# FFN weight conversion in a fused attention, MoE and FFT-mixer kernel: the product written over the raw words, the low parts subtracted by VectorE

## The chip, the cores and the metric

The kernel runs on one core of a Trainium2 chip. The metric is device microseconds (us) of one execution, the median of several runs. Engines are named as in the profile: PE (TensorE), DVE (VectorE), ACT (ScalarE), POOL (GpSimd), SP (SyncE, here only an issuer of DMAs).

## The reference

Three blocks follow one another on data of 4 batches, 576 rows and 512 columns: an attention, a gated MLP ("MoE"), and a Fourier mixer with a feed-forward network (FFN). The change touches only the preparation of the weights of the last block:

```python
def _moe2_ref(x, w_ch1, w_ch2):
    X = np.fft.fft(x, axis=1)
    X = np.fft.fft(X, axis=2)
    u = x + np.real(X).astype(np.float32)
    ...
    un = (u - mu) / np.sqrt(var + 1e-06)
    ch = np.maximum(un @ w_ch1, 0.0) @ w_ch2     # w_ch1: 512 x 2048, w_ch2: 2048 x 512
    return (u + ch).astype(np.float32)
```

The weights are drawn with numpy's default type, so `w_ch1` and `w_ch2` lie in memory as 8-byte floats, two 32-bit words for each number.

## The kernel before

Every product that must be exact to float32 is split: a number is a high part (rounded to the matmul's `fp32r` format) plus a low part, and `mm3` (L138) issues three matmuls (L139 high x high, L140, L141 with one low part each).

**The FFN's weights.** They are cut into 32 pieces of 128 x 512 numbers, one of `w_ch1` and one of `w_ch2` for each of the 16 steps `f` of the hidden dimension. A piece is fetched by SP as 128 x 1024 raw words (L921 for `w_ch1`, L113 for `w_ch2`) into one of 4 `raw` buffers, which lie in the space of the later tiles `unh` and `unl`. `narrow` (L118) makes float32 of it: ACT multiplies the odd words (the upper halves, taken as float32) by 2^-112 into a tile (L124); DVE shifts and masks that into a second tile (L125), ORs the sign in (L126), and ORs the top bits of the even words in (L128, which reads `raw` a second time and so is the last reader of the buffer). `split` (L105) then lets ACT write the rounded high part into its final place (L106) and an engine given by name subtract to get the low part (L107). For the FFN's pieces this engine was POOL, set by `W1ENG` and `W2ENG` (L83, L84). Both temporary tiles come from the ring `t2`, 6 buffers that the Fourier stages use too; in the trace a buffer of it is named `t`.

**When a piece is converted.** The converted pieces lie in tiles of the earlier stages, as these are released: `p_winh`, `p_winl`, `p_wsh`, `p_wsl`, and after the last Fourier transform `p_wfh`, `p_wfl`, `p_dsh`, `p_dsl`, `p_xgh`, `p_xgl`, `p_vyh`, `p_vyl` and others. The generator `ffn_gen` offers conversions (`ahead`, up to 3 steps ahead; `ready_w`, what is due; `conv_here`, at fixed places of the last batch's Fourier stages). After a piece is converted the fetch of the piece 4 further on is issued into its raw buffer.

**The FFN around it.** The rows are worked in five blocks. Of the first block, step `f` runs 12 matmuls of 512 columns for the hidden values of step f+1 (`ch1`, into a PSUM bank `mm`); ACT writes their high part `hh` (relu, L589), DVE the low part `hl` (L977, reading PSUM and `hh`); then 12 or more matmuls (`ch2`) multiply the `hh` and `hl` of step f with `w_ch2` into banks named `tp` and `sc`. The Fourier transform of the last batch (its stages `even`, `odd` and `tail`, L710 to L729, where DVE L727 writes a part of `yh`, and `even_d`, `odd_d` with DVE L815 to L822) runs between the first steps of that block. Only the first block meets conversions; the other four reuse the pieces.

**What sets the order.** The program text gives the dependencies; a scheduler at build time then fixes the order of the instructions on every engine, from the dependencies, the rings and its own model. Each engine runs its list in that order, so an instruction that waits holds all that stand behind it on its engine.

Of the kernel before, what the change touches and what calls it, by code (L numbers as in the profile page):

```python
# [44 lines left out]
def tile_attn_moe_fft_mixer(  # L45
# [18 lines left out]
    nc = tc.nc  # L64
# [15 lines left out]

    LOENG = nc.gpsimd
    E = {x: nc.gpsimd if x in POOLOPS else nc.vector for x in ('vnl', 'gl', 'pd', 'vd', 'un', 'vt', 'e', 'ed', 'pd1', 'wfl', 'bf', 'bf2', 'ul')}
    W1ENG = nc.gpsimd  # L83
    W2ENG = nc.gpsimd  # L84

    def bank(tag, shape):
        n = 1
# [10 lines left out]
    def t2(n=512):  # L98
        t = tmp.tile([P, 610], F32, tag="t2", name="t2", bufs=T2)
        return t[:, :n]  # L100
# [16 lines left out]

    def narrow(raw, n, scratch=None):  # L118
        w = raw.rearrange("p (n two) -> p n two", two=2)
        m = t2(n) if scratch is None else scratch[0]  # L120
        mi = m.bitcast(I32)
        a = t2(n) if scratch is None else scratch[1]
        ai = a.bitcast(I32)
        nc.scalar.mul(m, w[:, :, 1], 2.0 ** -112)  # L124
        nc.vector.tensor_scalar(ai, mi, 3, 0x7FFFFFF8, op0=ALU.logical_shift_left, op1=ALU.bitwise_and)  # L125
        nc.vector.scalar_tensor_tensor(ai, in0=mi, scalar=-2 ** 31, in1=ai, op0=ALU.bitwise_and,  # L126
                                       op1=ALU.bitwise_or)
        nc.vector.scalar_tensor_tensor(ai, in0=w[:, :, 0].bitcast(I32), scalar=29, in1=ai,  # L128
                                       op0=ALU.logical_shift_right, op1=ALU.bitwise_or)
        return a  # L130

    def split_raw(hi, lo, raw, n, dbl, eng):
        a = narrow(raw, n) if dbl else raw
        if len(hi.shape) == 3:
            a = a.rearrange("p (k m) -> p k m", k=hi.shape[1])
        split(hi, lo, a, eng)
# [50 lines left out]
    def prep():  # L187
        dbl = wide(w_in)
        sg = big.tile([P, 4, 512], F32, tag="wfl", name="scratch")
        prev = None  # L190
        for n in range(8):
            h, kk = 1 - n // 4, n % 4
            c = slice(h * 512, (h + 1) * 512)
            w = stage[n][:, :512 * dbl]
            if dbl == 2:
                w = narrow(w, 512, (sg[:, 2 * (n % 2), :], sg[:, 2 * (n % 2) + 1, :]))
            hi = winh[:, kk, c]
            nc.scalar.copy(hi, w)
            if prev is not None:
                prep_lo(*prev)  # L200
            prev = (winl[:, kk, c], w, hi)
            yield
        prep_lo(*prev)
        yield
# [39 lines left out]
    def prep_late():  # L244
# [8 lines left out]
        for kk in range(4):  # L253
            raw = stgs[kk % 2][:, :512 * dbl]
            w = narrow(raw, 512, (sg[:, 0, :], sg[:, 1, :])) if dbl == 2 else raw
            f = sg[:, 2, :]
            nc.vector.tensor_scalar(f[:, 0:257:256], w[:, 0:257:256], 2.0, None, op0=ALU.mult)
            nc.vector.tensor_tensor(f[:, 1:256], w[:, 1:256], w[:, 511:256:-1], op=ALU.add)
            nc.vector.tensor_tensor(f[:, 257:512], w[:, 1:256], w[:, 511:256:-1], op=ALU.subtract)
            if kk < 2:  # L260
                fetch(stgs[kk][:, :512 * dbl], w_out[(kk + 2) * P:(kk + 3) * P, :], nc.sync)
            nc.scalar.mul(wfh[:, kk, :], f, 0.25)
            nc.vector.scalar_tensor_tensor(wfl[:, kk, :], in0=f, scalar=0.25, in1=wfh[:, kk, :].bitcast(F32),
                                           op0=ALU.mult, op1=ALU.subtract)
            yield 0.5
# [644 lines left out]
    def ffn_gen(ffn):  # L910
# [13 lines left out]
        def conv_w(f, which):  # L924
            hi, lo = (w1, w2)[which][f]
            split_raw(hi, lo, raws[2 * (f % 2) + which][:, :512 * wd], 512, wd == 2, W1ENG if which == 0 else W2ENG)

# [154 lines left out]
    n = early = 0  # L1082
# [105 lines left out]
```

## Time and profile before

| | |
|---|---|
| time, median of 3 runs | 863.43 us (863.38 to 864.03) |
| the profiled execution: time, span in the trace | 863.25 us, 861.1 us |
| PE busy | 806.6 us, 94% of the span |
| DVE busy | 487.3 us, 57% |
| ACT busy | 304.0 us, 35% |
| POOL busy | 190.2 us, 22% |
| the chain that ended last, by engine | PE 77%, DVE 10%, SP's queue 5%, issue 3%, DMA 3%, ACT 1%, POOL 1% |
| TensorE's granted clock, mean | 0.98 of full speed |

All times in the profile are in us from the start of the span unless they are marked ns. A share such as "DVE 57%" is a mean over the whole span; the change touches only the stretch from about 393 us (the first piece) to 516 us (the last). The chain that ended last is followed backwards from the last instruction, each time to what released it. A row of the timeline names the start, the duration, the engine, the source line, the operation and its tiles; the brackets at its end say how long the engine had been idle just before it and what ended that. Consecutive instructions of one engine overlap a little in the records (an instruction's record ends some 0.08 us after the next one's begins), so what an instruction costs its engine is the distance between two starts.

### The profile page before, as it was taken

The page shows a single profiled execution, that of the slowest core. Times are in us where ns is not written, and L with a number is a line of the kernel's source. Part 1 is how long each engine was busy: PE and PEld are TensorE (multiplying, and loading weights), DVE is VectorE, ACT ScalarE, POOL GpSimd, SP SyncE. Part 2 cuts the span into 40 slices and gives each one's busy share as a digit, 9 for nine tenths or more (in the row PEclk, how much of TensorE's full clock was granted, in tenths as well). Part 3 has the DMA queues.
Part 4 walks back from the last instruction along what each step waited for, and adds up shares of the span by engine and source line. Part 5 has one row for each costly group of instructions (what it writes and reads, how often), then busy time and mean ns, then how long its engine had stood idle before and what let it go on. Part 6 is the DMA issues. An engine that isn't in the chain of part 4 may idle for free.

```text
span 861.1 us, 14356 instructions
## 1 busy us (share of the span) xinstructions
PE 806.6 (94%) x5309; PEld 667.6 (78%) x5309; DVE 487.3 (57%) x1109; ACT 304.0 (35%) x929; POOL 190.2 (22%) x237
## 2 busy tenths in 40 slices
PE   3758999999999999999798889999999999999998
PEld 1546888778977897889687658888888888888897
DVE  3798899577577846679959994223222322221211
ACT  1764674546373717434542542111110111111111
POOL 4447532224122310033623551000000000000000
PEclk9977999999999999999999999999999999999999
DMA  7789364432333110051525652322121222110100
GB/s 121 178 181 192 73 130 126 83 88 46 70 54 99 34 46 1 19 190 49 155 91 165 195 163 60 108 50 59 40 98 40 59 50 83 40 25 0 49 1 25
DMA packets 154210, 71.84 MB, mean 83 GB/s; under 512 B 122806, under 2 KB 140823, under 8 KB 154141
## 3 DMA queue, kind: packets, MB, share of 16 engines
q1 hardware_dynamic: 152668, 65.63, 31.2%
q0 software_dynamic: 1472, 5.30, 1.9%
q8 instruction: 42, 0.69, 0.3%
q14 instruction: 28, 0.22, 0.1%
HBM read 58.83 MB, written 12.07 MB: 82 GB/s over the span
## 4 chain that ended last, share of the span: by engine, by line
PE 77%; DVE 10%; SPq 5%; issue 3%; DMA 3%; ACT 1%; POOL 1%; DVEq 0%
PE mm L139 15%; PE mm L140 14%; PE mm L141 14%; PE tp L141 4%; PE tp L139 4%; PE tp L140 4%; PE sc L139 3%; PE sc L140 3%; PE sc L141 3%; SPq L326 3%; DVE t L128 2%; PE sc L433 2%; SPq L354 2%; PE sc L481 1%; DVE t L125 1%
## 5 line engine op out<-in xcount | busy, mean ns | idle before, releaser
L977 DVE SCALAR_TENSOR_TENSOR hl<-mm,hh 128x512 fp32r<-128x512 f32 (+1 forms) x80 | 50.9, 637 | 222.0 <-ACT hh L589 221.9
L589 ACT ACTIVATE hh<-mm 128x512 fp32r<-128x512 f32 (+1 forms) x80 | 44.3, 554 | 273.8 <-PE mm L141 269.2
L599 POOL TENSOR_TENSOR rs<-ve,nhalf 128x1 f32<-128x1 f32 (+1 forms) x38 | 25.2, 676 | 254.2 <-DVE ve L598 250.1
L386 ACT ACTIVATE eb<-sc,mx 128x64 f32<-128x64 f32 x140 | 41.7, 339 | 32.8 <-DVE mx L384 32.8
L139 PE MATMUL mm<-xgh,winh 128*128 128x288 f32 x128 | 39.2, 307 | 0.0
L139 PE MATMUL mm<-wsh,vnh 128*128 128x288 f32 x128 | 38.5, 301 | 0.0
L140 PE MATMUL mm<-xgl,winh 128*128 128x288 f32 x128 | 38.2, 298 | 0.0
L141 PE MATMUL mm<-xgh,winl 128*128 128x288 f32 x128 | 38.1, 297 | 0.0
L140 PE MATMUL mm<-wsl,vnh 128*128 128x288 f32 x128 | 38.0, 297 | 0.0
L141 PE MATMUL mm<-wsh,vnl 128*128 128x288 f32 x128 | 38.0, 297 | 0.0
L406 DVE STREAM_TRANSPOSE qk<-qk 128x576 f32<-128x576 f32 x28 | 21.7, 775 | 25.0 <-DMA qk<-in_q_dram 14.0
L128 DVE SCALAR_TENSOR_TENSOR t<-raw,t 128x512 int32<-128x512 int32 x32 | 34.6, 1085 | 0.1
L386 ACT ACTIVATION_READ_ACCUMULATOR eb<-sc,mx 128x1 f32 x140 | 32.4, 232 | 0.0
L423 POOL TENSOR_TENSOR ta<-qk 128x288 f32<-128x288 f32 x28 | 22.9, 817 | 41.0 <-DVE qk L406 34.3
L139 PE MATMUL mm<-wfh,xgh 128*128 128x512 f32 (+1 forms) x76 | 31.5, 414 | 0.0
L140 PE MATMUL mm<-wfl,xgh 128*128 128x512 f32 (+1 forms) x76 | 30.3, 400 | 0.0
L829 POOL DMA_INDIRECT u_d<-t,idx x12 | 15.5, 1293 | 64.8 <-DVE t L822 58.7
L141 PE MATMUL mm<-wfh,xgl 128*128 128x512 f32 (+1 forms) x76 | 29.4, 402 | 0.0
L481 PE MATMUL sc<-qk 64*64 64x64 f32 x560 | 20.4, 246 | 8.5 <-DMA qk<-in_q_dram 3.9
L481 PEld LDWEIGHTS sc<-qk 64*64 64x64 f32 x560 | 16.3, 153 | 14.6 <-DVE qk L406 9.8
L139 PE MATMUL mm<-winh,xgh 128*128 128x512 f32 x64 | 26.6, 416 | 0.7 <-DVE t L803 0.6
L411 POOL TENSOR_TENSOR vp<-vp 72x512 f32<-72x512 f32 x13 | 17.4, 1339 | 44.5 <-DMA vp<-in_v_dram 34.8
(535 smaller groups left out, 2542.8 us busy)
## 6 DMA issues: line engine op xcount, KB each, us to landing
raw<-in_moe_w_ch_dram SPq DMA_DIRECT2D x32, 512.0 KB
out_dram<-t SPq DMA_DIRECT2D x18, 256.0 KB
qk<-in_q_dram SPq DMA_DIRECT2D x56, 72.0 KB
qk<-in_k_dram SPq DMA_DIRECT2D x56, 72.0 KB
vp<-in_v_dram SPq DMA_DIRECT2D x26, 144.0 KB
vb<-in_v_dram SPq DMA_DIRECT2D x56, 64.0 KB
u2t<-u_d SPq DMA_DIRECT2D x10, 256.0 KB
t<-u_d SPq DMA_DIRECT2D x10, 256.0 KB
```

The costliest lines, as they stand in the source:

```text
L128: nc.vector.scalar_tensor_tensor(ai, in0=w[:, :, 0].bitcast(I32), scalar=29, in1=ai, op0=ALU.logical_shift_right, op1=ALU.bitwise_or)
L139: nc.tensor.matmul(out, lhsT=ah, rhs=bh, start=first, stop=False)
L140: nc.tensor.matmul(out, lhsT=ah, rhs=bl, start=False, stop=False)
L141: nc.tensor.matmul(out, lhsT=al, rhs=bh, start=False, stop=last)
L326: nc.sync.dma_start(x[pt:pt + 32].rearrange("p (j c) -> p j c", c=32), bass.AP(src.tensor, h * S * D + 32 * dh, [[D, 32], [32 * D, S // 32 ...
L386: nc.scalar.activation(e[:, i, :], sc[:, i, :], AF.Exp, bias=mx[:, i:i + 1], scale=sc_in, accum_out=sm[:, i:i + 1])
L406: nc.vector.transpose(x, x)
L423: E['pd'].tensor_tensor(a, x[:, 0::2], x[:, 1::2], op=ALU.add)
L481: nc.tensor.matmul(scs[u][c, z, :], lhsT=x[2 * hp][o, s:s + 64], rhs=x[2 * hp + 1][o, s:s + 64], start=False, stop=(i == 2 * m - 1 and hp ...
L589: nc.scalar.activation(dst, src, AF.Relu)
L599: nc.gpsimd.tensor_tensor(rs, ve, nhalf[:rows], op=ALU.pow)
L977: last[0] = nc.vector.scalar_tensor_tensor(hl[:, :n], in0=ph, scalar=0.0, in1=hh[:, :n].bitcast(F32), op0=ALU.max, op1=ALU.subtract)
```

## The change

Two edits in the code, one in each place:

```diff
-    W1ENG = nc.gpsimd
-    W2ENG = nc.gpsimd
+    W1ENG = nc.vector
+    W2ENG = nc.vector
...
     def narrow(raw, n, scratch=None):
         w = raw.rearrange("p (n two) -> p n two", two=2)
-        m = t2(n) if scratch is None else scratch[0]
+        m = w[:, :, 1] if scratch is None else scratch[0]
         mi = m.bitcast(I32)
         a = t2(n) if scratch is None else scratch[1]
```

The first edit moves the 32 subtractions L107 of the FFN's pieces from POOL to DVE. The second lets ACT (L124) write its product over the odd words of the raw buffer instead of into a `t2` tile, so a piece takes one buffer of the ring and not two; L125 and L126 then read that product with a stride of two words. Conversions with a `scratch` (those of the earlier stages' weights) stay as they were.

The scheduler also sets the instructions around the pieces in another order. In the lists that follow, a name with a number such as `t_5568` is one use of a `t2` buffer, and all operations on one such number belong to one piece.

ACT, around the second `hh` of the first block (the only L589 here), before:

```order
L106 CAST xgh<-t_5406 128x610
L106 CAST p_winl<-t_5424 128x512
L124 ACTIVATE t_5567<-raw 128x512
L124 ACTIVATE t_5588<-raw 128x512
L106 CAST p_winl<-t_5467 128x512
L106 CAST p_winl<-t_5531 128x512
L124 ACTIVATE t_5608<-raw 128x512
L106 CAST yh<-mm 128x258 x2
L106 CAST p_winl<-t_5568 128x512
L106 CAST p_wsh<-t_5589 128x512
L589 ACTIVATE hh<-mm 128x512
```

And after:

```order
L106 CAST xgh<-t_5402 128x610
L106 CAST p_winl<-t_5419 128x512
L106 CAST p_winl<-t_5461 128x512
L124 ACTIVATE raw<-raw 128x512
L589 ACTIVATE hh<-mm 128x512
L124 ACTIVATE raw<-raw 128x512
L106 CAST p_winl<-t_5524 128x512
```

Before, the casts of the pieces numbered 7 and 8 (counted from 0; `t_5568`, `t_5589`) stand ahead of this `hh`; after, the casts of pieces 4 and 5 (`t_5419`, `t_5461`) are the last ahead of it.

DVE, between two `hl` in the long stretch of conversions, before:

```order
L977 SCALAR_TENSOR_TENSOR hl<-mm,hh 128x512
L126 SCALAR_TENSOR_TENSOR t_6020<-t_6019,t_6020 128x512
L125 TENSOR_SCALAR t_6059<-t_6058 128x512
L128 SCALAR_TENSOR_TENSOR t_6020<-raw,t_6020 128x512
L126 SCALAR_TENSOR_TENSOR t_6059<-t_6058,t_6059 128x512
L125 TENSOR_SCALAR t_6068<-t_6067 128x512
L128 SCALAR_TENSOR_TENSOR t_6059<-raw,t_6059 128x512
L126 SCALAR_TENSOR_TENSOR t_6068<-t_6067,t_6068 128x512
L125 TENSOR_SCALAR t_6107<-t_6106 128x512
L977 SCALAR_TENSOR_TENSOR hl<-mm,hh 128x512
```

And after:

```order
L977 SCALAR_TENSOR_TENSOR hl<-mm,hh 128x512
L126 SCALAR_TENSOR_TENSOR t_5950<-raw,t_5950 128x512
L125 TENSOR_SCALAR t_5988<-raw 128x512
L125 TENSOR_SCALAR t_5996<-raw 128x512
L107 TENSOR_TENSOR p_xgh<-t_5942,p_xgh 128x512
L128 SCALAR_TENSOR_TENSOR t_5950<-raw,t_5950 128x512
L126 SCALAR_TENSOR_TENSOR t_5988<-raw,t_5988 128x512
L126 SCALAR_TENSOR_TENSOR t_5996<-raw,t_5996 128x512
L125 TENSOR_SCALAR t_6034<-raw 128x512
L128 SCALAR_TENSOR_TENSOR t_5988<-raw,t_5988 128x512
L977 SCALAR_TENSOR_TENSOR hl<-mm,hh 128x512
L107 TENSOR_TENSOR p_xgh<-t_5950,p_xgh 128x512
```

Before, eight conversion steps (three for each piece) stand between these two `hl`; after, nine of four for each piece, the subtraction among them.

ACT, at the last batch's first evacuations from PSUM (L589 into `t`, L647), before:

```order
L589 ACTIVATE t_4978<-mm 128x512
L589 ACTIVATE t_5004<-mm 128x512
L589 ACTIVATE t_5030<-mm 128x512
L647 COPY t_5056<-mm 64x512
L106 CAST unh<-av 128x4x128
```

And after:

```order
L589 ACTIVATE t_4978<-mm 128x512
L124 ACTIVATE raw<-raw 128x512
L589 ACTIVATE t_5004<-mm 128x512
L124 ACTIVATE raw<-raw 128x512 x2
L589 ACTIVATE t_5030<-mm 128x512
L124 ACTIVATE raw<-raw 128x512
L647 COPY t_5056<-mm 64x512
L106 CAST unh<-av 128x4x128
```

The first four products, which no longer need a buffer of the ring, now stand between these evacuations.

## Rows read from the trace of the kernel before

**Rows 1.** Windows: length, busy of PE, PEld, DVE, ACT, POOL, clock, DMA share, GB/s.

```profile
430.00:440.00 10.00, 10.00 (x39) 7.69 (x38) 7.43 (x11) 5.72 (x15) 5.15 (x4) 0.79 0.62 198
...
480.00:490.00 10.00, 9.11 (x40) 6.93 (x39) 10.00 (x14) 4.89 (x8) 4.53 (x5) 1.00 0.62 195
490.00:500.00 10.00, 6.92 (x28) 4.72 (x27) 10.00 (x13) 5.03 (x8) 5.64 (x4) 1.00 0.62 179
500.00:510.00 10.00, 7.00 (x28) 5.05 (x27) 10.00 (x13) 5.61 (x9) 5.05 (x4) 0.96 0.61 189
510.00:520.00 10.00, 9.96 (x38) 7.67 (x37) 9.28 (x14) 2.87 (x6) 5.08 (x5) 0.86 0.46 135
```

**Rows 2.** Windows again, the rest of the FFN.

```profile
560.00:860.00 300.00, 296.96 (x1375) 244.37 (x1373) 73.68 (x135) 39.29 (x71) 5.47 (x10) 1.00 0.17 44
```

**Rows 3.** Waits of PE from 370 to 560: total, times, longest.

```profile
PE tp L139 <- ACT hh L589: 7.1, 3, 5.0
PE tp L141 <- DVE hl L977: 4.8, 3, 1.9
PE mm L139 <- DVE t L816: 2.3, 1, 2.3
```

**Rows 4.** Timeline of ACT, around the second `hh`.

```profile
427.13 0.62 ACT L106 CAST p_winl<-t 128x512 fp32r<-128x512 f32 x1 [2.12 <-DVE t L128]
...
428.26 0.59 ACT L589 ACTIVATE hh<-mm 128x512 fp32r<-128x512 f32 x1
```

**Rows 5.** Timeline of PE: the matmul after that `hh`.

```profile
428.90 0.79 PE L139 MATMUL tp<-p_winh,hh 128*128 128x512 f32 x1 [5.04 <-ACT hh L589]
```

**Rows 6.** Timeline of DVE: the L128 of piece 5.

```profile
419.21 0.68 DVE L128 SCALAR_TENSOR_TENSOR t<-raw,t 128x512 int32<-128x512 int32 x1
```

**Rows 7.** Timeline of DVE: steps of pieces, between two `hl` four steps apart.

```profile
482.18 0.68 DVE L977 SCALAR_TENSOR_TENSOR hl<-mm,hh 128x512 fp32r<-128x512 f32 x1
...
500.90 0.41 DVE L125 TENSOR_SCALAR t<-t 128x512 int32<-128x512 int32 x1
501.23 1.78 DVE L128 SCALAR_TENSOR_TENSOR t<-raw,t 128x512 int32<-128x512 int32 x1
502.93 0.68 DVE L126 SCALAR_TENSOR_TENSOR t<-t,t 128x512 int32<-128x512 int32 x1
...
514.66 0.68 DVE L977 SCALAR_TENSOR_TENSOR hl<-mm,hh 128x512 fp32r<-128x512 f32 x1
```

**Rows 8.** Timeline of POOL, the subtractions of the same stretches.

```profile
417.44 4.54 POOL L107 TENSOR_TENSOR p_winl<-t,p_winl 128x512 fp32r<-128x512 f32 x1 [2.76 <-ACT p_winl L106]
...
501.10 1.36 POOL L107 TENSOR_TENSOR p_vyh<-t,p_vyh 128x512 fp32r<-128x512 f32 x1 [1.28 <-ACT p_vyh L106]
```

**Rows 9.** Timeline of PE: the first matmul of two successive steps.

```profile
479.47 0.39 PE L139 MATMUL mm<-unh,p_wfh 128*128 128x512 f32 x1
...
485.08 0.39 PE L139 MATMUL mm<-unh,p_wfl 128*128 128x512 f32 x1
```

**Rows 10.** Lines by form: busy, mean ns of one, idle before.

```profile
L107 DVE TENSOR_TENSOR vnl<-t,vnh 128x512 fp32r<-128x512 f32 x16 | 10.7, 685 | 0.4 <-ACT vnh L106 0.4
```

**Rows 11.** Timeline of DVE: in the last Fourier stage, and a piece's L126 later.

```profile
455.40 0.42 DVE L821 TENSOR_TENSOR t<-t,t 128x255 f32<-128x255 f32 x1
...
456.06 1.48 DVE L821 TENSOR_TENSOR t<-t,t 128x255 f32<-128x255 f32 x1
...
474.71 1.79 DVE L126 SCALAR_TENSOR_TENSOR t<-t,t 128x512 int32<-128x512 int32 x1
```

**Rows 12.** Timeline of SP's queue, two fetches.

```profile
373.33 0.35 SPq L113 DMA_DIRECT2D raw<-in_moe_w_ch_dram  x1
...
497.81 0.38 SPq L921 DMA_DIRECT2D raw<-in_moe_w_ch_dram  x1
```

**Rows 13.** Timeline of ACT, an evacuation of the last batch, and a product.

```profile
377.94 0.58 ACT L647 COPY t<-mm 64x512 f32<-64x512 f32 x1 [1.74 <-PE av L965]
...
501.58 0.66 ACT L124 ACTIVATE t<-raw 128x512 f32<-128x512 f32 x1 [0.56 <-DMA raw<-in_moe_w_ch_dram]
```

## The prediction

> **What bounds the kernel now.** I read the windows first. From 560 to 860 PE is busy 296.96 of 300 us at a full clock [rows 2], so that part is a queue of matmuls: it neither gains from the change nor gives anything back, and what is saved earlier reaches the end whole. The conversions run from about 393 to 516. In that stretch the waits of PE are three groups [rows 3]: 7.1 us for `hh`, of them one wait of 5.04 [rows 5]; 4.8 for `hl`; 2.3 for a DVE step of the last Fourier stage. To these comes the clock: from 430 to 440 it is 0.79, from 500 to 510 it is 0.96, from 510 to 520 it is 0.86, each behind a stretch in which PE sat idle, while full PE work elsewhere in these windows shows 1.00 [rows 1]. So all that can be won is 14.2 us of idle time and a few us of clock.
>
> Then I ask who makes PE wait. In the last third of the conversions DVE is busy 10.00 of 10 us in three windows running, and PE drops to 9.11, 6.92 and 7.00 [rows 1]. DVE is the bound there. The timeline shows why [rows 7]: L125 starts 0.33 ahead of L128, a L126 has 0.68 in its record, which is 0.60 to the next start, but L128 takes 1.70 to the next start. It begins 0.13 after POOL's subtraction of 1.36 [rows 8], and 1.36 - 0.13 + 0.60 is 1.83: it looks as if it stood still until POOL was done. The same L128 took 0.68 at 419.21 [rows 6]. There POOL is the one held: its subtraction from 417.44 lasts 4.54 [rows 8]. A piece costs DVE 0.60 + 0.33 + 1.70 = 2.63 beside POOL, and four steps from `hl` to `hl` take 514.66 - 482.18 = 32.5 us, 8.1 each [rows 7], while PE's work for a step is 485.08 - 479.47 = 5.61 [rows 9].
>
> **The change, part by part.**
>
> *The subtraction on DVE.* It adds 32 steps to DVE. The same form on DVE (128 x 512, from `t` and a high part) has a mean of 0.685 [rows 10], and as records overlap by 0.08 it costs 0.60. What it removes is POOL's work beside DVE. In the last third a piece then costs L125 0.33 and three steps of 0.60: 2.13 against 2.63. Between two `hl` the order has nine steps (before, eight), three of them L125: 3 x 0.33 + 6 x 0.60 = 4.6, and 0.60 for `hl`, 5.2 us. That is under PE's 5.61, so PE sets the pace, and `hl` keeps its lead. Gone are the idle time of 480 to 510, 0.89 + 3.08 + 3.00 = 6.97 [rows 1], and the clock behind it, 10 x 0.04 + 10 x 0.14 = 1.8: 8.77 together, 8.7 in the sum. The pieces that the slower rhythm leaves over (two or three each step, where three went before) run in later steps, under the same cover.
>
> *The first third.* The second `hh` starts at 428.26 on ACT, behind the cast of 427.13, which waited 2.12 for a L128 [rows 4]; in the order of before these casts are those of pieces 7 and 8. PE needs it at 428.90 - 5.04 = 423.9 [rows 5]. In the order of after the last cast ahead of it is that of piece 5. Before, piece 5 was through its L128 at 419.21 + 0.60 = 419.8 [rows 6]. With four subtractions ahead of it on DVE, 4 x 0.60 = 2.4, and no relief from POOL at all, that is 422.2, then two ACT steps of 0.6: `hh` begins by 423.4 and is done by 424.0; with relief a us or two earlier. So the wait of 5.04 goes, and the clock that fell behind it, 10 x 0.21 in 430 to 440 [rows 1] and half of the 1.1 us before, 2.6, with it: 7.5, a little taken off.
>
> What is late next there is DVE's part of `yh` (L727), for which PE's next-but-one group waits. From the second `hl`, at about 421.8 if DVE gets relief, the order has twelve steps of 0.60, three L125 and some 1.4 us of short ones: 7.2 + 1.0 + 1.4 = 9.6, done at 431.4. PE comes to it after 36 long matmuls of 5.61 / 24 = 0.234 and six short ones, from 423.9 about 432.9. A margin of 1.5 that is worked out over 9.6 us is thin; I put 0.5 us of new wait there.
>
> *The middle.* Behind the wait of 2.3 for L816 [rows 3] stands L821, which took 1.48 beside POOL where the one before took 0.42 [rows 11]: 1.06 goes. One subtraction comes into this place, 0.60. I take 0.5, up to 1.7 with the clock.
>
> *The product over the raw words.* ACT's L124 costs what it did (it writes as many words). L125 and L126 now read with a stride. L126 keeps 0.60, as L128 shows, whose raw operand has this stride already [rows 6]. No row shows a L125 with a stride: it is between the 0.33 of the contiguous one and the 0.60 of a step with two tensor operands [rows 7]. I take 0.33, and 0.60 as the other end. At that end the nine steps and `hl` take 10 x 0.60 = 6.0 for a step, 0.4 over PE's pace; over eight steps 3 us. Worked back from the order, `hl` goes into this stretch about 6 us ahead of PE and would be 3 us ahead at its end, so the last third holds; the margin at L727 does not (rival A).
>
> [...]
>
> *Buffers.* A piece holds one ring buffer, not two, so L124 no longer waits for an old subtraction. It holds its raw buffer no longer than before, since L128 was its last reader already. The four products that now stand between the evacuations of the last batch could hold these back: the fetch issued at 373.33 [rows 12], at the 3.8 us that a later one took (497.81 to 501.58 [rows 12, 13]), lands at about 377.1, and the evacuation behind it began at 377.94 [rows 13]. With 0.6 for the product it loses at most 1.3, and PE has other banks filled: nothing is taken.
>
> **The sum**, on the profiled execution of 863.25 (its span is 861.1): - 7.5 (first third) - 0.5 (middle) - 8.7 (last third) + 0.5 (L727) = 847.05. That execution lies 0.18 under the median of the runs, so the forecast is **847.2**.
>
> **The rivals.**
>
> *A: the first third gives part back.* If L125 takes 0.60, or the relief from POOL is small, DVE is 1 to 4 us later at L727, and PE waits 2 to 4 us there with some clock behind it, or `hh` is late again by part of the 5.04: 849.5 to 853. For: the thin margin. Against: steps that POOL stretches, as the 1.79 of one L126 [rows 11], end there too.
>
> *B: half of the last third comes back.* ACT's list is in order, and an `hh` behind a product whose fetch is late waits with it; at 501.58 a product did wait for its fetch [rows 13]. If such waits take up half of the 8.7, and some of the clock: 853 to 858.
>
> *C: slower.* The long L128s could come from reading `raw` with a stride while matmul operands and DMAs move (the DMA share is 0.62 there [rows 1]), not from POOL. Then they stay, and DVE, which is full, gets the subtractions on top: about 31 x 0.60 = 18.6, less the 2 it idles: 863.4 + 17 = 880. It decides from the point at which a piece costs DVE more than 2.5 without POOL. Against: the L128 of 0.68 [rows 6], and an L126 with contiguous operands that took 1.79 while POOL worked [rows 11].
>
> [...]
>
> *D: nothing.* The idle time turns up as other waits (the fetches, or conversions that come due): 863, within 1.7 us.
>
> **How the numbers follow.** Chances: the forecast 0.60 (843.5 to 849.5), A 0.20 (849.5 to 853), B 0.09 (853 to 858), C 0.04, D 0.04, and 0.03 for under 843.5, were all three waits to go with all of the clock. The range leaves out C, D, the upper half of B and the low end: **843.5 to 855**. A measurement of this kernel can tell about 0.2%, 1.7 us, from no change. Faster by more: forecast, A, B and the low end, 0.92; within: D less a share, 0.03; slower: C and that share, 0.05.
>
> **What would show it.** In the changed kernel's profile: L128 and L126 at about 0.68 everywhere, and POOL near zero from 393 to 516 (else C); L125 at 0.41 as a record (else A); the matmul after the second `hh` without a long wait, and L764's wait for `yh` under 1 us (else A); `hl` to `hl` at 5.6 in the steps after the Fourier stages, no wait of PE for L977, and the clock at 1.00 there (else B). I am wrong if PE's idle time between 420 and 520 is over half of what it was.

## The result and the profile after

The changed kernel takes 851.70 us (median of 4 runs, 848.91 to 852.45) against 863.58 of the kernel before in the same comparison (863.38 to 864.03); the ratio is 0.9862, 95% interval 0.9836 to 0.9888. The forecast was 847.2, its range 843.5 to 855. The time lies inside the range and 4.5 us above the forecast: outside the 843.5 to 849.5 that I had given a chance of 0.60, and where rival A had been put (849.5 to 853, chance 0.20). The direction and the main mechanism were right. The profiled execution took 851.31, its span is 849.5, 11.6 less than before.

The waits of PE from 370 to 560, in the changed kernel (total, times, longest), answer to [rows 3]:

```profile
PE mm L139 <- ACT yx L729: 2.2, 1, 2.2
PE mm L139 <- DVE t L816: 1.8, 1, 1.8
PE mm L139 <- ACT t L589: 1.4, 1, 1.4
PE mm L139 <- DVE t L648: 0.8, 1, 0.8
PE mm L139 <- ACT unh L106: 0.7, 1, 0.7
PE mm L140 <- DVE unl L107: 0.4, 1, 0.4
PE tp L139 <- ACT hh L589: 0.4, 1, 0.4
```

The 7.1 for `hh` are down to 0.4 and the 4.8 for `hl` are gone. But in place of three groups with 14.2 us there are seven with 7.7, and five of them are new: L729 in the tail of the Fourier stage, L589 and L648 at the last batch's evacuations, `unh` and `unl` at the start of the second block.

Windows of the changed kernel (length, busy of PE, PEld, DVE, ACT, POOL, clock, DMA share, GB/s), to be held against [rows 1]:

```profile
370.00:380.00 10.00, 9.30 (x48) 7.47 (x46) 5.67 (x18) 3.46 (x6) 2.69 (x4) 1.00 0.86 280
380.00:390.00 10.00, 8.60 (x64) 8.37 (x65) 7.48 (x20) 5.14 (x12) 1.61 (x3) 1.00 0.03 11
...
420.00:430.00 10.00, 10.00 (x45) 7.90 (x44) 10.00 (x20) 6.02 (x16) 0.00 (x0) 1.00 0.60 208
430.00:440.00 10.00, 7.80 (x40) 6.42 (x39) 7.58 (x15) 7.69 (x18) 0.00 (x0) 0.96 0.63 209
440.00:450.00 10.00, 10.00 (x53) 8.37 (x51) 2.33 (x5) 2.47 (x5) 0.00 (x0) 0.87 0.01 3
...
480.00:490.00 10.00, 10.00 (x44) 8.09 (x43) 8.81 (x17) 5.26 (x10) 0.00 (x0) 1.00 0.59 185
490.00:500.00 10.00, 10.00 (x44) 8.09 (x43) 8.88 (x17) 4.94 (x9) 0.00 (x0) 1.00 0.63 199
500.00:510.00 10.00, 9.63 (x42) 7.54 (x41) 9.71 (x20) 5.54 (x10) 1.05 (x1) 1.00 0.72 210
```

From 480 to 510 PE is full where it had 6.97 us of idle time, and DVE, at 8.81 to 9.71, is under its limit with a step more in each piece. The costliest rows by form (busy, mean ns of one, idle before) say why:

```profile
L128 DVE SCALAR_TENSOR_TENSOR t<-raw,t 128x512 int32<-128x512 int32 x32 | 21.7, 682 | 0.0
L126 DVE SCALAR_TENSOR_TENSOR t<-raw,t 128x512 int32<-128x512 int32 x32 | 21.6, 682 | 0.0
L125 DVE TENSOR_SCALAR t<-raw 128x512 int32<-128x512 int32 x32 | 13.3, 419 | 5.2 <-ACT raw L124 4.5 <-DMA u_d<-t,idx 0.6
L124 ACT ACTIVATE raw<-raw 128x512 f32<-128x512 f32 x32 | 21.7, 677 | 34.6 <-DMA raw<-in_moe_w_ch_dram 34.5
```

L128 and L126 are at 0.68 each, with a stride too, and the strided L125 is at 0.42 as a record, the contiguous price. The last row is the one to stop at: the products now wait 34.5 us for their fetches, where they waited 10.7 in the kernel before. That is idle time of ACT; it costs where something that PE wants stands behind it (2.1 us at the evacuations, below).

**The two places where time is lost.** The first is at the last batch's evacuations. SP and ACT, timeline:

```profile
373.19 0.35 SPq L113 DMA_DIRECT2D raw<-in_moe_w_ch_dram  x1
```

```profile
375.75 0.67 ACT L124 ACTIVATE raw<-raw 128x512 f32<-128x512 f32 x1 [2.67 <-DMA raw<-in_moe_w_ch_dram]
376.33 0.58 ACT L589 ACTIVATE t<-mm 128x512 f32<-128x512 f32 x1
...
379.46 0.65 ACT L124 ACTIVATE raw<-raw 128x512 f32<-128x512 f32 x1 [1.99 <-DMA raw<-in_moe_w_ch_dram]
380.02 0.58 ACT L589 ACTIVATE t<-mm 128x512 f32<-128x512 f32 x1
381.21 0.67 ACT L124 ACTIVATE raw<-raw 128x512 f32<-128x512 f32 x1 [0.61 <-DMA raw<-in_moe_w_ch_dram]
381.90 0.58 ACT L647 COPY t<-mm 64x512 f32<-64x512 f32 x1
```

ACT's list is in order, so each evacuation waits behind a product that waits for a fetch. The fetch issued at 373.19 let its product go at 381.21, after 8.0 us; the one before it, issued at 369.96, at 379.46, after 9.5. L647 begins at 381.90, 4 us after [rows 13], and PE idles 0.70 + 1.40 = 2.1 us in the windows from 370 to 390, behind these evacuations.

The second place is the tail of the Fourier stage. DVE, ACT and PE, timeline:

```profile
434.96 0.42 DVE L727 TENSOR_TENSOR yh<-mm,yh 32x256 fp32r<-32x256 f32 x1
435.41 0.69 DVE L128 SCALAR_TENSOR_TENSOR t<-raw,t 128x512 int32<-128x512 int32 x1
```

```profile
435.76 0.40 ACT L106 CAST xgh<-mm 128x290 fp32r<-128x290 f32 x1 [0.70 <-PE mm L764]
436.05 0.66 ACT L124 ACTIVATE raw<-raw 128x512 f32<-128x512 f32 x1
436.62 0.60 ACT L106 CAST p_wsh<-t 128x512 fp32r<-128x512 f32 x1
437.12 0.36 ACT L728 COPY yx<-mm 33x256 f32<-33x256 f32 x1
437.50 0.37 ACT L729 COPY yx<-mm 33x257 f32<-33x257 f32 x1
```

```profile
437.92 0.40 PE L139 MATMUL mm<-dsh,yh 128*128 128x290 f32 x1 [2.20 <-ACT yx L729]
```

L727 ends before PE wants its result, but the two copies that free the PSUM bank stand on ACT behind a product and behind the cast of a piece that PE first reads at 459.6. No fetch holds this product; it only takes its turn. PE waits 2.20, and the clock goes to 0.96 and 0.87 in the two windows behind it (0.4 + 1.3 us).

### The profile page after: what moved, and what is told of

It is laid out like the page before. It is cut to its first block, busy times and chain, and to the rows that moved or that the text cites. A ratio compares the mean times of both kernels' runs of the same rounds, so it can differ in the third digit from the quotient of the medians.

```text
span 849.5 us, 14317 instructions
## 1 busy us (share of the span) xinstructions
PE 800.5 (94%) x5309; PEld 664.6 (78%) x5309; DVE 478.5 (56%) x1141; ACT 302.4 (36%) x929; POOL 141.3 (17%) x205
## 4 chain that ended last, share of the span: by engine, by line
PE 75%; DVE 9%; DMA 7%; SPq 4%; ACT 3%; issue 2%; POOL 1%; DVEq 0%; ACTq 0%
PE mm L139 15%; PE mm L140 14%; PE mm L141 14%; PE tp L139 4%; PE tp L140 4%; PE tp L141 4%; DMA raw<-in_moe_w_ch_dram 4%; PE sc L139 3%; PE sc L140 3%; PE sc L141 3%; SPq L326 2%; PE sc L433 2%; PE av L458 1%; PE sc L481 1%; PE av L512 1%
## 5 line engine op out<-in xcount | busy, mean ns | idle before, releaser
L977 DVE SCALAR_TENSOR_TENSOR hl<-mm,hh 128x512 fp32r<-128x512 f32 (+1 forms) x80 | 50.9, 636 | 222.5 <-ACT hh L589 222.5
L589 ACT ACTIVATE hh<-mm 128x512 fp32r<-128x512 f32 (+1 forms) x80 | 44.3, 554 | 268.4 <-PE mm L141 263.9
L139 PE MATMUL mm<-xgh,winh 128*128 128x288 f32 x128 | 39.5, 308 | 2.1 <-ACT t L589 1.4
L139 PE MATMUL mm<-wsh,vnh 128*128 128x288 f32 x128 | 38.5, 301 | 0.0
L829 POOL DMA_INDIRECT u_d<-t,idx x12 | 16.1, 1338 | 110.3 <-DVE t L822 104.2
L124 ACT ACTIVATE raw<-raw 128x512 f32<-128x512 f32 x32 | 21.7, 677 | 34.6 <-DMA raw<-in_moe_w_ch_dram 34.5
L139 PE MATMUL mm<-wfh,xgh 128*128 128x512 f32 (+1 forms) x76 | 31.1, 409 | 0.0
L139 PE MATMUL mm<-winh,xgh 128*128 128x512 f32 x64 | 26.5, 415 | 0.7 <-DVE t L822 0.6
L383 DVE TENSOR_REDUCE mx<-sc 72x2 f32<-72x288 f32 (+2 forms) x49 | 24.3, 506 | 4.9 <-PE sc L433 4.2
L139 PEld LDWEIGHTS mm<-xgh,winh 128*128 128x128 f32 x128 | 24.1, 188 | 3.5 <-ACT t L589 1.6
```

Of the source, the lines that this page charges most:

```text
L139: nc.tensor.matmul(out, lhsT=ah, rhs=bh, start=first, stop=False)
L383: nc.vector.reduce_max(mx, sc, axis=AX.X)
L589: nc.scalar.activation(dst, src, AF.Relu)
L977: last[0] = nc.vector.scalar_tensor_tensor(hl[:, :n], in0=ph, scalar=0.0, in1=hh[:, :n].bitcast(F32), op0=ALU.max, op1=ALU.subtract)
```

## The experiments

To compare traces, two instants are taken from each timeline: the start of L729 in the tail of batch 2 (counted from 0, so the last batch is 3), which lies ahead of anything the change touches (341.4 to 347.6 in these traces: what lies ahead of it varies from one execution to the next), and the starts of the `hl` (L977), of which the 16th closes the first block. All in us; the ratio is to the kernel before in the same comparison.

| kernel | time, median | ratio, 95% interval | tail of batch 2 to first `hl` | to the 16th | to the last | all |
|---|---|---|---|---|---|---|
| before | 863.58 | | 68.9 | 126.9 | 315.2 | 511.0 |
| changed | 851.70 | 0.9862 (0.9836 to 0.9888) | 69.0 | 113.5 | 317.1 | 499.6 |
| changed, again | 850.50 | 0.9854 (0.9832 to 0.9876) | 68.4 | 112.7 | 317.1 | 498.2 |
| first edit alone | 844.66 | 0.9806 (0.9782 to 0.9831) | 66.0 | 111.8 | 317.2 | 494.9 |
| second edit alone | 864.80 | 1.0039 (1.0015 to 1.0062) | 69.3 | 128.8 | 315.2 | 513.3 |
| POOL busy beside | 859.17 | 0.9969 (0.9950 to 0.9988) | 70.2 | 121.1 | 317.1 | 508.3 |
| first products gated | 850.55 | 0.9877 (0.9855 to 0.9899) | 68.2 | 112.5 | 317.1 | 497.8 |
| tail first | 850.11 | 0.9856 (0.9837 to 0.9875) | 66.8 | 114.5 | 317.2 | 498.5 |
| both of these | 851.92 | 0.9890 (0.9875 to 0.9906) | 69.8 | 112.5 | 317.1 | 499.5 |
| products late | 846.62 | 0.9806 (0.9780 to 0.9832) | 65.9 | 113.1 | 317.1 | 496.2 |
| first edit, tail first | 845.50 | 0.9810 (0.9793 to 0.9828) | 66.0 | 111.1 | 317.1 | 494.2 |
| half of the first edit | 848.61 | 0.9822 (0.9796 to 0.9848) | 67.2 | 113.2 | 315.2 | 495.5 |
| before, pieces spread | 856.40 | 0.9939 (0.9921 to 0.9957) | 68.9 | 118.0 | 317.1 | 504.0 |

**Each edit alone.** The first:

```diff
-    W1ENG = nc.gpsimd
-    W2ENG = nc.gpsimd
+    W1ENG = nc.vector
+    W2ENG = nc.vector
```

> The first edit alone: DVE subtracts the low parts, the product still goes into a ring tile. Theory (POOL beside DVE was the cost): L128 and L126 at 0.68, PE's waits for hl near zero, and since no product stands between the evacuations of the last batch, the waits of 1.35 and 0.75 at 380 to 383 are absent: 847 to 852 us. Rival (the ring's relief by the product in place is what gained): 858 to 864 us, with L124 waiting for ring buffers.

and the second:

```diff
-        m = t2(n) if scratch is None else scratch[0]
+        m = w[:, :, 1] if scratch is None else scratch[0]
```

> The second edit alone: the product is written over the raw words, POOL still subtracts. Theory (POOL beside DVE was the cost): L128 or L126 stay stretched to 1.1 us or more as a mean, PE's waits for hl stay: 857 to 865 us. Rival (the ring's relief gained): 848 to 853 us.

The first edit alone takes 844.66: it gains more than the two together, and more than its theory gave (847 to 852). The second alone is a little slower than before. The waits of PE with the first edit alone, 370 to 560:

```profile
PE mm L139 <- DVE t L816: 1.8, 1, 1.8
PE mm L139 <- ACT yx L729: 1.1, 1, 1.1
PE mm L139 <- ACT unh L106: 0.7, 1, 0.7
PE mm L140 <- DVE unl L107: 0.4, 1, 0.4
```

The waits at the evacuations are absent, as expected, and the one for L729 is half as long. With the second edit alone PE still waits 4.7 us for `hl`, and the rows by form show POOL's stretch still there, with L128 reading the same words (a mean of 1.00, a little under the 1.1 that I expected):

```profile
L128 DVE SCALAR_TENSOR_TENSOR t<-raw,t 128x512 int32<-128x512 int32 x32 | 31.6, 997 | 0.0
L126 DVE SCALAR_TENSOR_TENSOR t<-raw,t 128x512 int32<-128x512 int32 x32 | 23.3, 737 | 0.0
```

So the ring's relief gains nothing, and the whole gain is the first edit's.

**Was it POOL?** POOL gets as many operations of the size back, which read a high part twice and write a tile that nobody reads; DVE's list between any two `hl` has the same number of conversion steps as in the changed kernel.

```diff
-        split(hi, lo, a, eng)
+        split(hi, lo, a, eng), (beside(hi) if dbl and eng is nc.vector else None)
+    beside = lambda hi: nc.gpsimd.tensor_tensor(dm[0]..., hi.bitcast(F32), hi.bitcast(F32), op=ALU.subtract)
```

> The changed kernel, and beside each subtraction on DVE POOL does one of the same size (of a high part with itself, into a tile nobody reads), so that the contention is back while DVE's work stays as in the changed kernel. Theory (contention): L128, L126 and L107 are stretched again, 1.0 us or more as a mean where POOL works, DVE becomes the bound from 464 to 516 with four steps a piece, and the time is 862 to 885 us. Rival (it was the work's place, order or the ring): within 2 us of the changed kernel, 850 to 854 us.

Against the changed kernel of the same comparison (850.50) POOL's busy work costs 8.7 us; from tail to last `hl` it is 8.7 and 10.1 against that kernel's two traces. The rival's 850 to 854 is out, but the size is short of the theory's 862 to 885: L128 has a mean of 0.80, L126 of 0.79. The dose was smaller than I meant it to be: POOL's busy operation takes 1.04 at its shortest, where the subtraction of the kernel before took 1.28, and all in all it stretches the pieces' steps on DVE by about 16 us, where the subtractions had stretched them by about 23. The place is not the one that I expected either. Of the 8.7 us, 5.9 are lost ahead of PE's first `ch1` matmul (L139) with `p_wsh` as its high part, most of them in the tail of the Fourier stage:

```profile
PE mm L139 <- ACT yx L729: 4.9, 1, 4.9
```

The last third loses 2.8; from 480 to 510 PE idles 1.56 us, not the 6.97 of [rows 1]. So POOL's work beside DVE is shown to cost, but with nine steps between two `hl` this dose of it does not bring the old last third back.

In the timeline of POOL and of DVE in this kernel

```profile
496.50 1.27 POOL L137 TENSOR_TENSOR dm<-p_xgh 128x512 bf16<-128x512 f32 x1 [3.59 <-ACT p_xgh L106]
497.85 1.37 POOL L137 TENSOR_TENSOR dm<-p_xgl 128x512 bf16<-128x512 f32 x1
```

```profile
496.79 0.68 DVE L977 SCALAR_TENSOR_TENSOR hl<-mm,hh 128x512 fp32r<-128x512 f32 x1
497.39 0.92 DVE L107 TENSOR_TENSOR p_xgh<-t,p_xgh 128x512 fp32r<-128x512 f32 x1
498.24 1.52 DVE L128 SCALAR_TENSOR_TENSOR t<-raw,t 128x512 int32<-128x512 int32 x1
```

the `hl` of 496.79, which reads PSUM, runs its 0.68 in the middle of POOL's first operation; the subtraction behind it, with two operands in SBUF, ends late (0.92, where the same form alone has a mean of 0.685 [rows 10]), and L128 takes 1.52 beside POOL's second. Both end 0.54 after the operation of POOL that they met (497.77 and 499.22). The POOL row of 4.54 in [rows 8] shows the other order: there DVE's step had begun 0.14 earlier (417.30); DVE went through six steps without a gap, and POOL's record ends 1.15 after the last of them.

**Half the dose.** Only `W1ENG` is changed.

```diff
-    W1ENG = nc.gpsimd
+    W1ENG = nc.vector
```

> A half dose of the first edit: DVE subtracts for w_ch1, POOL still for w_ch2; the product goes into a ring tile as before. Theory (POOL beside DVE is the cost): each subtraction of POOL still stretches a DVE step by about 1 us, half as often: L128 and L126 with a mean of about 0.8, and 850 to 857 us, about halfway between 844.7 and 862. Rival (the gain comes from the order that the scheduler makes when POOL is out of it, or from POOL's late low parts): a jump, 844 to 847 or 860 and more.

848.61: neither theory's number. L128 comes to 0.73 and L126 to 0.77, as the theory has it, but at half the dose nine tenths of the gain are there (ratio 0.9822 against 0.9806). That suggests that the price of a stretch is not a sum over operations: it counts where DVE's work for a step passes PE's 5.6 us. This run alone does not show it: its order also puts two or three pieces between two `hl` of the last third, where the kernel before mostly has three, and the mean granted clock of its profiled execution is 0.988, where the runs of the kernel before in that comparison show 0.968 to 0.987.

**Spread instead of moved.** If so, the kernel before could be helped with POOL where it is. From piece 16 on its pieces are put behind the `hl`s, two for each:

```diff
-LA, LN, CC, CO = 3, (2, 1), 1.5, 1.0
+LA, LN, CC, CO = 1, (2, 1), 1.5, 1.0
...
-            split_raw(hi, lo, ...
+            with (tc.issue_after(last[0].ins) if 2 * f + which >= 16 else nullcontext()): split_raw(hi, lo, ...
```

> The kernel before (POOL subtracts, the product in a ring tile), but from piece 16 on the steps of a piece are queued behind the hl that is last written in the program, and pieces are offered one step ahead instead of three: DVE then has six conversion steps (two pieces) between two hl in the last third, where the kernel before has eight to ten (three pieces). Theory (in the last third the loss is POOL's stretch times three pieces a step, and three come from an order made without that stretch): a step takes DVE 2 x 2.63 + 0.60 = 5.9 against PE's 5.6, so of the 6.97 of idle time and 1.8 of clock some 2 stay: 856 to 858.5 us. Rival (the stretch costs the same however the pieces are spread): 861 to 865 us. A third (pieces put off come too late): over 865.

856.40 lies in what the theory gave. The windows of this kernel:

```profile
480.00:490.00 10.00, 9.54 (x41) 7.13 (x40) 8.46 (x13) 4.57 (x8) 4.02 (x4) 1.00 0.52 175
490.00:500.00 10.00, 10.00 (x44) 7.74 (x43) 7.99 (x13) 4.99 (x9) 4.87 (x4) 1.00 0.64 212
500.00:510.00 10.00, 8.82 (x38) 6.54 (x36) 8.34 (x15) 5.14 (x9) 5.58 (x5) 1.00 0.48 155
```

POOL is as busy as before, yet PE idles 1.64 us from 480 to 510, where it had 6.97. So in the last third the loss was POOL's stretch times three pieces in a step. The first edit helps there twice: it ends the stretch, and with four steps to a piece the scheduler's nine steps between two `hl` hold fewer pieces.

That the total fits is in part luck. Counted from the tail of batch 2, PE's first `ch1` matmul (L139) with `p_wsh` as its high part comes 4.3 us earlier than in the kernel before, the first with `p_vyh` 12.8 earlier, and the last `hl` 7.0 earlier. The 4.3 are won ahead of the last third, where the theory had nothing: the wait for L816 is 0.2 and not 2.3, and the clock behind it is 1.00. The last third gives 8.5, and 5.8 are lost behind it, where the last pieces are late and PE waits, among others, 2.8 us for `unl` and `unh` at the start of the second block.

**What the second edit costs.** Two attempts to undo its two visible waits, alone and together. The gate puts the first four products behind L647 on ACT:

```diff
-                nc.scalar.copy(vt, pv[n:])
+                gate[0] = nc.scalar.copy(vt, pv[n:])
...
-        nc.scalar.mul(m, w[:, :, 1], 2.0 ** -112)
+        with (tc.issue_after(gate[0].ins) if scratch is None else nullcontext()): nc.scalar.mul(...)
```

> The changed kernel with the first four products queued on ACT behind the last evacuation of batch 3 (L647), nothing else. Theory (the products ahead of the evacuations wait for fetches that land late, and PE waits for the evacuations): the waits for t L589 and t L648 at 380 to 384 go, 2.1 us of them, and the pieces behind them are 2 to 3 us earlier: 847.5 to 849.5 us. Rival (these waits are hidden by what is late later): as the changed kernel, 850 to 852 us.

The other puts all work of pieces 8 and later behind L727 on DVE and L729 on ACT (`tl` holds these two instructions):

```diff
-            split_raw(hi, lo, ...
+            with (tc.issue_after(tl[0].ins) ...), (tc.issue_after(tl[1].ins) ...): split_raw(hi, lo, ...
```

> The changed kernel with the work of pieces 8 and later queued on DVE and ACT behind the last steps of the Fourier stage's tail (L727, L729), nothing else. Theory (DVE and ACT work of pieces that are not yet needed stands ahead of L727 and L729): the wait of 2.20 for L729 goes and with it most of the clock that falls behind it, 2 to 4 us: 847 to 849 us. Rival (the pieces that are put off become late and hh or hl waits, or another bank is late): 850 to 854 us.

> Both of these queueings in the changed kernel. Theory (the second edit costs only by where the scheduler then puts the steps): the two gains add to 4 to 6 us, 845 to 847 us, as fast as the first edit alone (844.66). Rival (the product in place costs something of its own, as a stride or a later fetch): 848 us or more.

All three theories missed: 850.55, 850.11, 851.92, each in its rival's range and none clearly apart from the changed kernel. Each wait went and another came. With the gate, ACT and PE show

```profile
410.31 0.66 ACT L124 ACTIVATE raw<-raw 128x512 f32<-128x512 f32 x1 [1.35 <-DMA raw<-in_moe_w_ch_dram]
410.88 0.68 ACT L106 CAST xgh<-t 128x610 fp32r<-128x610 f32 x1
```

```profile
411.62 0.50 PE L139 MATMUL av<-wfh,xgh 128*128 128x512 f32 x1 [2.01 <-ACT xgh L106]
```

a later product now stands, waiting for its fetch, ahead of a cast that PE wants. With the tail first, four products stand in a row on ACT behind L729 and ahead of a cast of `yh`, and PE waits 2.3 for the copy L717 that follows from this cast by way of DVE, where it had waited 2.2 for L729. These four products do not wait for a fetch; they take about 0.6 each of ACT's time. It is the same fault at other places (a product that waits, or merely takes its turn, ahead of something that PE wants), which speaks for the order and against a price of the product itself, but does not show it. So a last version kept the product in place and took ACT's order from the first edit alone: products 0 and 1 behind the last evacuation into `u`, 2 to 7 behind the casts of the parts of `xgh`.

```diff
+            with (tc.issue_after(gate[(0, 0, 1, 2, 3, 3, 4, 4)[min(seen(scratch), 7)]].ins) if scratch is None else nullcontext()): nc.scalar.mul(...)
...
+                gate[:] = [relu_evac(u[:, f, c], pu)]
```

> The changed kernel with the first eight products queued on ACT where the first edit alone has them: 0 and 1 behind the last evacuation into u, 2 to 7 behind the casts of the four parts of xgh. From the tail of batch 2 (L729 at about 343) to the last hl the first edit alone took 494.9 us, the changed kernel 499.6 and 498.2, and most of this lies ahead of the first hl of the FFN: 66.0 against 69.0 and 68.4 from the tail of batch 2. Theory (the product in place frees ACT's list of the ring, so products are placed earlier, and they wait there for fetches ahead of work that PE needs): the first hl comes 65.5 to 66.5 after the tail of batch 2, all in all 494.5 to 496.5, and the time is 844.5 to 847. Rival (the product in place costs by itself, as strided reads or as raw buffers that are held longer): the first hl at 68 or later and 850 us or more.

846.62, with 65.9 to the first `hl` and 496.2 in all, each inside what the theory gave. The time to the first `hl` is that of the first edit alone (66.0). The product in place costs nothing in itself there; it costs where it is then put. What is left of the difference (1.3 us from tail to last `hl`) is of the size of the wait for L729, which is still 2.2 here and 1.1 in the first edit alone.

**The changed kernel again, and the best of both.**

> The changed kernel itself, for a second trace of it: its four runs lie 3.5 us apart. Theory (the products behind late fetches move with the landing of these fetches): the waits at 375 to 390 and the idle before L124 for DMA differ between the two traces by a us or two, the rest agrees. Rival (the late step of the last Fourier stage varies): the wait of 2.20 for L729 is another.

The wait for L589 is absent in this trace, that for L648 is 1.3, and L729's is 2.2 again: the waits behind fetches move by a microsecond, the late copy does not. The two traces differ by 1.4 us from tail to last `hl`, of which 0.7 is PE's idle time from 370 to 390 (2.1 and 1.4).

> The first edit alone, with the queueing behind the tail. Theory: the wait of 1.14 for L729 goes, with some of the clock behind it (0.91 from 440 to 460): 842 to 844 us, faster than both kernels of the case. Rival (put off pieces are late): 844.5 to 848 us.

845.50: the wait for L729 is gone, and L816's has grown from 1.8 to 2.4. It cannot be told from the first edit alone (ratios 0.9810 and 0.9806). The theory's 842 to 844 is missed. The first edit alone, 844.66, has the lowest median of the study, 0.98 of the kernel before.

## Why the prediction was right, and where it was short

- *DVE's steps without POOL.* Right: L128 and L126 at 0.68, and L125 with a stride at 0.42 as a record (forecast: 0.41). That it would be the lower end of 0.33 to 0.60 was my estimate; no row of before showed it. Rival C (the stride is the cause) falls with these rows.
- *The first third.* Right: the second `hh` began at 423.60 (I had "by 423.4"), the wait of 5.04 is gone (0.4 is left) and the clock in 420 to 430 is 1.00.
- *The last third.* Right in size: idle time 6.97 to 0.37, clock back at 1.00, 8.4 against 8.7. The reason that I put first, the shorter piece, is half of it: three pieces of 2.13 and an `hl` would still take DVE 7.0 us a step (an estimate from [rows 7]), over PE's 5.61. What brings it under is that nine steps between two `hl` hold fewer than three pieces. The prediction has this in its 5.2 us a step, but names it only in passing.
- *The middle.* Under-sized: the wait for L816 fell from 2.3 to 1.8, as forecast, but the clock behind it came back too. The windows of the kernel before

```profile
450.00:460.00 10.00, 7.71 (x55) 6.98 (x54) 8.82 (x25) 1.04 (x2) 2.43 (x2) 0.90 0.30 96
460.00:470.00 10.00, 10.00 (x42) 8.05 (x41) 8.89 (x20) 4.67 (x8) 3.37 (x4) 0.92 0.56 169
```

  lose 1.0 + 0.8 us to it, those of the changed kernel show 1.00 there: 2.3 us against 0.5.
- *The clock.* Not as steady as I wrote it. The sum has 2.6 us of clock behind the wait for `hh` and 1.8 behind the last third, as if such idle time always brought a fall. With the second edit alone PE idles 6.74 us from 480 to 510, nearly as in the kernel before, and the windows at its end and behind it read

```profile
500.00:510.00 10.00, 7.11 (x29) 4.79 (x27) 10.00 (x13) 4.94 (x9) 4.54 (x5) 1.00 0.63 196
510.00:520.00 10.00, 7.93 (x32) 5.90 (x33) 9.93 (x15) 4.00 (x7) 4.95 (x4) 1.00 0.48 156
```

  where [rows 1] have 0.96 and 0.86. With the first edit alone the wait for L816 is 1.8, as in the changed kernel, and the window behind it falls to 0.83, where the changed kernel shows 1.00:

```profile
450.00:460.00 10.00, 10.00 (x38) 7.96 (x37) 8.84 (x24) 4.82 (x8) 1.83 (x2) 0.83 0.60 184
```

  So the clock terms are those of one execution of each kernel, and how much of them is the change's is not shown. That they came out, and that of the middle came on top, is in part luck.
- *The late step at L727.* The term that failed most: 0.5 taken, 2.2 + 1.7 = 3.9 found. I followed DVE alone. DVE got no relief there (10.00 of 10 from 420 to 430), the second `hl` came at 424.29 and not at 421.8, and L727 at 434.96 and not by 431.4; even so PE did not wait for its result. What it waited for were L728 and L729 on ACT. In the kernel before these follow L727 at once:

```profile
438.47 0.42 DVE L727 TENSOR_TENSOR yh<-mm,yh 32x256 fp32r<-32x256 f32 x1 [1.40 <-ACT yh L726]
```

```profile
438.93 0.37 ACT L728 COPY yx<-mm 33x256 f32<-33x256 f32 x1 [0.49 <-DVE yh L727]
```

  By this distance of 0.46 L728 could have begun at 435.4 in the changed kernel; it began at 437.12, behind a cast of `xgh`, a product and the cast of a piece. So some 1.7 of the 2.2 are ACT's order, and some 0.5 are L727's own lateness (an estimate from these rows). The size is rival A's (849.5 to 853), its reason, a late DVE, is the smaller part.
- *The product over the raw words, "nothing is taken".* Failed: 2.1 us of idle time at the evacuations in the profiled execution (1.4 in the second trace), and 4.7 and 3.3 from tail to last `hl` against the first edit alone. The step that failed is the landing of the fetch: I took 3.8 us from a fetch at 497.81 [rows 12, 13], where the DMA share is 0.62; four fetches issued between 368 and 373 lie among loads and stores of the last batch (DMA share 0.86 and 280 GB/s from 370 to 380), and the third took 9.5, the fourth 8.0. The bound of 1.3 that I gave was one product's, and there were four.
- *Not foreseen:* 1.1 us of waits at the start of the second block, for `unh` and `unl`, which the order now puts right ahead of their first matmul. They come with the first edit alone too. So not all that is saved earlier reaches the end, unlike what I wrote: the column "to the last" is 1.9 longer than before, and these waits are 1.1 of that.

Together: - 7.6 (first third) - 2.3 (middle) - 8.4 (last third) + 3.9 + 2.1 + 1.1 = - 11.2, against 11.6 between the spans; 4.5 of the 11.2 are clock. PE's idle time between 420 and 520 is 4.3 us, where it was 14.3, well under the half at which I would have been wrong. The part that the first edit makes alone, 511.0 - 494.9 = 16.1 from tail to last `hl`, is what I had forecast for both, and in much the same parts: counted from the tail of batch 2, PE's first `ch1` matmul (L139) with `p_winl` as its high part comes 6.7 us earlier than before (forecast for the first third with L727: 7.0), that with `p_wsh` 7.1 (forecast with the middle: 7.5), the last `hl` 16.1 (16.2).

## To carry to other kernels

A buffer that a ring no longer holds back does not only save a wait: a scheduler will place its producer earlier, and on an engine that works its list in order a producer that waits for a DMA holds everything behind it, as here at the evacuations (2.1 us of idle time of PE), and one that does not wait still takes its turn ahead of it, as here at L729 (2.2); ask for each moved instruction what stands behind it, and take the landing time from a stretch with the same DMA load (here 3.8 us in one stretch, 8.0 and 9.5 in another). Work that slows another engine should be costed by the pace of the stretch (steps per period times the stretched price against the period of the bound engine), not by the operation, and spreading it can win a part of what moving it wins (here 7.0 of 16.1 us). When a change has two edits, price each by itself: here the one that looked free took back over a quarter of the gain.

## What the runs showed of the hardware

A piece's step on DVE that began while a subtraction of POOL was under way was held until that ended, unless DVE held that subtraction itself, as it did the one of 4.54 [rows 8]. In the kernel before there are 20 such steps L126 and L128, with two operands in SBUF: each ends 0.54 to 0.56 us after POOL's record, from 0.83 us with 0.28 of POOL's operation left to 1.79 with 1.23 left [rows 11]; alone they take 0.68. L125, with one operand, was held too, four times for 1.50 to 1.53, where it takes 0.41 alone. An `hl`, which reads one operand from PSUM, was not held: 0.68 at 496.79 inside a POOL operation of 1.27, and 0.67 or 0.68 in all five such cases of that trace. So in these 20 rows POOL's price for DVE is what is left of its operation when the step begins, less 0.13 (0.68 - 0.55). POOL's busy work, which reads one array twice and writes 2-byte values, is shorter (1.04 against 1.28 at the shortest) and held a step to 1.53 at most. A 512 KB fetch took 3.8 us at a DMA share of 0.62, and 8.0 and 9.5 in a stretch at 0.86 (280 GB/s).
